# Larger and smaller buffer pools, and a precomputed product spread over more tiles, in a fused attention and two-MLP kernel

## The chip, the cores and the metric

The kernel runs on one core of a Trainium2 chip. Its time is device microseconds, as a median over runs. Everything is one program: an attention step and two MLPs over 4352 tokens, in float32.

## The reference, cut to what matters

```python
# attention: x [8, 8, 512, 64], state [8, 8, 32, 64]
a  = softmax(x @ state^T / 8);      xread = a @ state        # tokens read the state
a2 = softmax(state @ x^T / 8);      sread = a2 @ x           # the state reads the tokens
x  = concatenate([xread, sread], axis=2)                     # -> [4352, 512]
# first MLP, w_in [512, 2048], w_out [2048, 512]
h = x @ w_in
g = where(h >= 1, h, where(h <= -1, 0, (h + 1)**2 / 4))
x = g @ w_out
# second MLP, the same sizes
h = x @ w_in2
g = maximum(h, 0) + alpha * minimum(h, 0)
return g @ w_out2
```

The weights arrive as float64, and the kernel turns their words into float32 itself. Most matrix products are made of three matmuls each: both operands are split into a high part (a cast on ACT) and a low part (a subtraction on DVE), and high x high, high x low and low x high are added up in PSUM.

## The kernel before, in words

**First MLP.** Tokens are worked in nine tiles: tile t below 8 holds the 512 tokens of batch t, tile 8 the 256 rows that the state has read. A tile has 16 steps, one for each 128 columns of the hidden layer; step number i is 16 t + f. In step i the code issues the hidden-layer matmuls of step i + 2 (`h_mm`, L560), the activation on ACT and DVE, and the output matmuls of step i (`out_mm`, L602). All other work hangs on step numbers through `at(i, ...)` (L992): the attention of the next batch, weights and transfers.

For tokens that read the state, the hidden layer is not x @ w_in but attention weights times V, where V = state @ w_in is made ahead: 32 rows for each batch and head. V is made for two groups of batches: batches 1 to 4 during tile 0 (`vg_dir`, L503), and the later batches' V by `vg_plan` (L1043). That plan has 32 products, one for each of 4 column blocks and 8 heads. Product n hangs on step `start + int(n * per)`, with start at step 32, the first step of tile 2: two steps ahead its weights are loaded on POOL's queue into a 2 KB tile (`vg_load`, L493), one step behind it two matmuls go into a PSUM bank (`vg_mm`, L511), ACT copies the bank to SBUF and SP's queue stores it to DRAM (`vg_out`, L498). Batch by batch V comes back from DRAM (`vr_load`, L520), 8 loads a tile, from eight steps into the tile before on.

The raw x of a batch is loaded twice for each half of the heads: as `x1` (L125, four loads of 128 KB) and as `x2` (L134, one of 512 KB). ACT casts x2 to its high part `x2h` (L232, in `s5`).

From step 36 on the weights of the second MLP are prepared too (`w2_plan`, L1084): every 3.4 steps a raw load of 512 KB, decoding, sums of quarters on POOL, high and low parts, and stores to DRAM on SP's queue (`put`, L667).

**Second MLP.** It uses the seven-product scheme for 2 x 2 blocks (Strassen's in Winograd's form) in both layers. The tokens are worked in five super-tiles of two halves of 448 or 416 tokens. For each, the hidden layer comes first (56 units of 6 matmuls: 8 column blocks by 7 products), then the product stage of the output (56 units of 6 matmuls), with a few units of either interleaved at the seams (`second`, L932). The raw input of the next super-tile is loaded in units 4 to 7 of the product stage (`xr_load`, L728; four loads, each of two 128-row slices side by side), combined in place by four subtractions or additions (`x_comb`, L736) and split into high and low parts (`x_split`, L745), from unit 11 on. The seven products of the output need 8 slices each, a high and a low part of 448 columns in one 4 KB tile (`o_split`, L831). The code asks for slice m + 5 in unit m; the first product's 8 slices and 4 of the second's are made during the hidden layer. A slice is free again after its second unit; the first two slices of a product after its third unit.

**Buffers and order.** `U` tiles (128 x 512 words, 2 KB in each partition) come from one pool of 72, `V` tiles (4 KB) from a pool of 14 (L43 and L44). V tiles hold x, x2h and x2l, raw weights, put buffers, the raw input `xr`, slices `gs` and output tiles `ot`. The order on each engine is made when the program is built: of the instructions that are ready the earliest in the code goes first, and a tile is given a buffer when one is free. On the chip every engine and SP's queue work through their list in that order.

Of the kernel before, what the change touches and what calls it, by code (L numbers as in the profile page):

```python
# [14 lines left out]
ALU = mybir.AluOpType  # L15
# [24 lines left out]
@with_exitstack  # L40
def kernel_body(ctx: ExitStack, tc: tile.TileContext, x, state, w1i, w1o, w2i, w2o, alpha, out):
    nc = tc.nc
    up = ctx.enter_context(tc.tile_pool(name="up", bufs=72))  # L43
    vp = ctx.enter_context(tc.tile_pool(name="vp", bufs=14))  # L44
    cp = ctx.enter_context(tc.tile_pool(name="cp", bufs=1))
    sp = ctx.enter_context(tc.tile_pool(name="sp", bufs=4))
    pa = ctx.enter_context(tc.tile_pool(name="pa", bufs=4, space=bass.MemoryType.PSUM))
# [3 lines left out]
    def U(name, dt=F32):  # L51
        return up.tile([128, 512], dt, tag="u", name=name)

    def V(name, dt=F32):
        return vp.tile([128, 1024], dt, tag="v", name=name)
# [7 lines left out]
    act, dve, pool, pe, ld = nc.scalar, nc.vector, nc.gpsimd, nc.tensor, nc.sync  # L63
# [8 lines left out]
    def hi_(h, raw):  # L72
        act.copy(h, raw)  # L73

    def lo_(l, raw, h, eng=None):
        (eng or dve).tensor_tensor(out=l, in0=raw, in1=h.bitcast(F32), op=ALU.subtract)  # L76
# [18 lines left out]
    xd = dp.tile([NO, 128, TOK], F32, name="xd")  # L95
# [456 lines left out]
    def gi(t, f):  # L552
        return t * NF + f
# [166 lines left out]
    WS, XR, XB, HB, GT, GR, GS, OA, OC, OS = {}, {}, {}, {}, {}, {}, {}, {}, {}, []  # L720
# [4 lines left out]
    def wof(s):  # L725
        return HALF[s]

    def xr_load(s, kh, tk):  # L728
        w = wof(s)
        v = V(f"xr{s}{kh}{tk}")[:, :2 * w]  # L730
        c0 = BASE[s] + tk * w
        ld.dma_start(out=v.rearrange("p (k c) -> p k c", k=2),
                     in_=xd[2 * kh:2 * kh + 2, :, c0:c0 + w].rearrange("k p c -> p k c"))
        XR[s, kh, tk] = v

    def x_comb(s, m):  # L736

        b11, b21, b12, b22 = [XR[s, kh, tk] for tk in range(2) for kh in range(2)]
        x, y, op = {3: (b22, b12, ALU.subtract), 2: (b12, b11, ALU.add),
                    4: (b21, b11, ALU.subtract), 1: (b22, b11, ALU.subtract)}[m]  # L740
        dve.tensor_tensor(out={3: b12, 2: b11, 4: b21, 1: b11}[m], in0=x, in1=y, op=op)

    XAT = [11, 13, 18, 20, 22, 33, 35, 37, 42, 44, 46]

    def x_split(s, p):  # L745
        w = wof(s)
        b11, b21, b12, b22 = [XR[s, kh, tk] for tk in range(2) for kh in range(2)]
        src = {0: b11, 1: b21, 2: b22, 3: b21, 4: b11, 5: b11, 6: b12}[p]
        for kk in range(2):
            h, l = U(f"xh{s}{p}{kk}", F32R)[:, :w], U(f"xl{s}{p}{kk}", F32R)[:, :w]  # L750
            r = src[:, kk * w:(kk + 1) * w]
            hi_(h, r)
            lo_(l, r, h)
            XB[s, p, kk] = (h, l)

    XSTEPS = [(x_split, 0), (x_comb, 3), (x_split, 1), (x_comb, 2), (x_split, 5), (x_comb, 4),
              (x_split, 3), (x_comb, 1), (x_split, 4), (x_split, 6), (x_split, 2)]

    def w1_get(s, q, p):
# [172 lines left out]
    def second():  # L932
# [23 lines left out]
        for n, (kind, s, a, b) in enumerate(ev):  # L956
# [6 lines left out]
            if kind == "h":  # L963
                h_item(s, a, b)
                h_after(s, a, b)
                next(late, None)
                if b == 3:
                    o_split(s, 0, a)
                if b == 6 and a in (1, 3, 4, 6):
                    k = (a - 1) // 2 + a // 4  # L970
                    o_split(s, 1, k)
                    g_comb(k, 4)
            else:
                m = 8 * a + b
                if 12 <= m + 5 < 56:
                    o_split(s, *divmod(m + 5, 8))
                if 8 <= m < 12:
                    g_comb(m - 4, 4)
                if 23 <= m < 31:
                    g_comb(m - 23, 1)  # L980
                if s + 1 < NSUP and 4 <= m < 8:
                    xr_load(s + 1, m % 2, m // 6)
                o_item(s, a, b % 4 // 2, [b // 4 * 4 + b % 2 * 2 + k for k in range(2)])
                if s + 1 < NSUP and m in XAT:
                    fn, arg = XSTEPS[XAT.index(m)]
                    fn(s + 1, arg)
# [5 lines left out]
    def at(i, fn, *a):  # L992
        side[i].append((fn, *a))
# [49 lines left out]
    def vg_plan(g, start, per):  # L1043
        n = 0
        for blk in range(4):
            for h in range(NH):
                o = start + int(n * per)
                at(o - 2, vg_load, g, blk, h)
                at(o + 1, vg_mm, g, blk, h)
                n += 1  # L1050
        at(start - 2, ld_stg, g)
        at(start, st_build, g, 0)
        at(start, st_build, g, 1)
# [4 lines left out]
    for blk in range(4):  # L1058
        for c in range(4):
            at(max(1 + c, 4 * blk - 5 + c), vg_dir, blk, c)  # L1060
    vg_plan(1, gi(2, 0), 1.0)

    for blk in (1, 2, 3):
        for c in range(4):
# [37 lines left out]
    for k in range(4):  # L1102
        at(gi(7, 12), xr_load, 0, k % 2, k // 2)
# [88 lines left out]
```

## Time and profile before

| | us |
|---|---|
| three timed runs | 1413.91, 1421.23, 1421.24 |
| their median | 1421.23 |
| the profiled execution's own time | 1414.61 |
| its span in the trace | 1412.8 |
| PE busy in the span | 1374.0 (97%) |
| DVE busy | 1066.7 (75%) |
| ACT busy | 821.3 (58%) |
| POOL busy | 101.9 (7%) |

The span runs from the first to the last instruction of the program in the trace; the 1.8 us between it and the execution's own time lie outside. PE's busy time is the time in which any matmul is in flight, so it tells where PE starves but not whether it works at its best pace. The clock that was granted to PE is told for each stretch as a share of full speed. Busy shares of DVE, ACT and POOL are means over stages with different limits.

### The profile page before, as it was taken

The page shows a single profiled execution, that of the slowest core. Times are in us where ns is not written, and L with a number is a line of the kernel's source. Part 1 is how long each engine was busy: PE and PEld are TensorE (multiplying, and loading weights), DVE is VectorE, ACT ScalarE, POOL GpSimd, SP SyncE. Part 2 cuts the span into 40 slices and gives each one's busy share as a digit, 9 for nine tenths or more (in the row PEclk, how much of TensorE's full clock was granted, in tenths as well). Part 3 has the DMA queues.
Part 4 walks back from the last instruction along what each step waited for, and adds up shares of the span by engine and source line. Part 5 has one row for each costly group of instructions (what it writes and reads, how often), then busy time and mean ns, then how long its engine had stood idle before and what let it go on. Part 6 is the DMA issues. An engine that isn't in the chain of part 4 may idle for free.

```text
span 1412.8 us, 20324 instructions
## 1 busy us (share of the span) xinstructions
PE 1374.0 (97%) x6596; PEld 1192.7 (84%) x6596; DVE 1066.7 (75%) x1896; ACT 821.3 (58%) x1586; POOL 101.9 (7%) x123
## 2 busy tenths in 40 slices
PE   6799999998999999999999999999999999999998
PEld 4466688886788888888898999899999999999997
DVE  6878596776769797976678796779677868786873
ACT  5567676665677776775565454545454545463552
POOL 1000002231222111112111000000000000000000
PEclk9999999999999999999999999999999999999999
DMA  6898446488875656656777786878677777779765
GB/s 200 308 320 272 121 86 146 124 232 239 214 223 160 170 156 191 175 168 197 263 263 259 250 291 192 263 224 279 202 251 255 237 232 255 257 243 308 227 226 159
DMA packets 295962, 312.28 MB, mean 221 GB/s; under 512 B 144048, under 2 KB 179888, under 8 KB 295856
## 3 DMA queue, kind: packets, MB, share of 16 engines
q1 hardware_dynamic: 255504, 293.09, 65.8%
q0 software_dynamic: 33280, 8.51, 3.2%
q10 hardware_dynamic: 7072, 9.37, 1.9%
q8 instruction: 53, 0.87, 0.3%
q14 instruction: 53, 0.43, 0.1%
HBM read 237.90 MB, written 72.35 MB: 220 GB/s over the span
## 4 chain that ended last, share of the span: by engine, by line
PE 83%; issue 5%; DMA 4%; DVE 3%; ACT 2%; POOL 1%; SPq 1%; POOLq 0%; ACTq 0%; DVEq 0%
PE accB L855 23%; PE hB L780 22%; PE accA L620 18%; PE hA L84 11%; PE accA L612 3%; PE vgp L84 1%; DMA vd<-vgo 1%; PE sr L84 1%; PE sc L84 1%; DMA x<-in_x_dram 1%; DMA w2d<-wo 1%; PE vdp L84 1%; DMA wr_wi<-in_moe_w_in_dram 0%; PE vgp L516 0%; PE et L205 0%
## 5 line engine op out<-in xcount | busy, mean ns | idle before, releaser
L855 PE MATMUL accB<-gs,wv 128*128 128x448 f32 (+1 forms) x1680 | 334.8, 359 | 0.5 <-ACT o L873 0.5
L855 PEld LDWEIGHTS accB<-gs,wv 128*128 128x128 f32 x1680 | 315.1, 188 | 16.5 <-ACT o L873 0.8
L780 PE MATMUL hB<-xh,wu 128*128 128x448 f32 (+1 forms) x1120 | 318.4, 361 | 3.0 <-ACT p L806 0.8
L780 PEld LDWEIGHTS hB<-xh,wu 128*128 128x128 f32 x1120 | 210.2, 188 | 18.4 <-ACT p L806 2.3
L780 PE MATMUL hB<-xl,wu 128*128 128x448 f32 (+1 forms) x560 | 201.3, 359 | 0.0
L73 ACT CAST gs<-c 128x448 fp32r<-128x448 f32 (+1 forms) x200 | 109.1, 556 | 79.1 <-PE accB L855 56.1
L787 ACT ACTIVATE m<-c 128x448 f32<-128x448 f32 (+1 forms) x120 | 68.2, 568 | 118.0 <-DVE c L802 115.3
L588 DVE SCALAR_TENSOR_TENSOR g<-y,hA 128x512 f32<-128x512 f32 (+1 forms) x144 | 93.5, 649 | 51.0 <-ACT y L586 49.9
L76 DVE TENSOR_TENSOR gs<-c,gs 128x448 fp32r<-128x448 f32 (+1 forms) x200 | 114.8, 602 | 5.8 <-ACT gs L73 5.0
L76 DVE TENSOR_TENSOR gl<-g,gh 128x512 fp32r<-128x512 f32 (+1 forms) x128 | 88.7, 693 | 36.0 <-ACT gh L73 28.4
L789 DVE SCALAR_TENSOR_TENSOR c<-m,beta_sb,c 128x448 f32<-128x448 f32 (+1 forms) x120 | 80.9, 674 | 44.7 <-ACT m L787 42.3
L585 ACT ACTIVATE y<-hA 128x512 f32<-128x512 f32 (+1 forms) x144 | 82.3, 572 | 52.8 <-PE hA L84 51.2
L780 PEld LDWEIGHTS hB<-xl,wu 128*128 128x128 f32 x560 | 105.2, 188 | 5.1
L73 ACT CAST gh<-g 128x512 fp32r<-128x512 f32 (+1 forms) x128 | 75.7, 592 | 38.4 <-DVE g L588 34.8
L586 ACT ACTIVATE y<-y 128x512 f32<-128x512 f32 (+1 forms) x144 | 87.6, 608 | 3.9
L829 DVE TENSOR_TENSOR c<-c,c 128x448 f32<-128x448 f32 (+1 forms) x120 | 71.9, 612 | 1.9
L802 DVE TENSOR_TENSOR c<-hB,u 128x448 f32<-128x448 f32 (+1 forms) x80 | 48.5, 607 | 25.5 <-PE hB L780 14.6
L500 ACT COPY vgo<-vgp 128x512 f32<-128x512 f32 x64 | 37.2, 586 | 50.4 <-PE vgp L84 23.7
L612 PE MATMUL accA<-g,wf_w1o 128*128 128x512 f32 x128 | 61.0, 607 | 4.6 <-DVE wf_w1o L405 4.6
L76 DVE TENSOR_TENSOR gs<-m,gs 128x448 fp32r<-128x448 f32 (+1 forms) x80 | 47.0, 601 | 16.2 <-ACT gs L73 16.2
L73 ACT CAST gs<-m 128x448 fp32r<-128x448 f32 (+1 forms) x80 | 43.1, 556 | 25.2 <-PE accB L855 20.4
L612 PEld LDWEIGHTS accA<-g,wf_w1o 128*128 128x128 f32 x128 | 24.4, 193 | 26.2 <-issue 18.8
(961 smaller groups left out, 2820.0 us busy)
## 6 DMA issues: line engine op xcount, KB each, us to landing
wu<-w1d SPq DMA_DIRECT2D x280, 256.0 KB
wv<-w2d SPq DMA_DIRECT2D x280, 256.0 KB
vd<-vgo SPq DMA_DIRECT2D x64, 256.0 KB
vr<-vd SPq DMA_DIRECT2D x56, 256.0 KB
w1d<-wu SPq DMA_DIRECT2D x56, 256.0 KB
w2d<-wo SPq DMA_DIRECT2D x40, 256.0 KB
x<-in_x_dram SPq DMA_DIRECT2D x18, 512.0 KB
wr_wi<-in_moe_w_in_dram SPq DMA_DIRECT2D x16, 512.0 KB
```

Source lines behind the costliest of these rows:

```text
L73: act.copy(h, raw)
L76: (eng or dve).tensor_tensor(out=l, in0=raw, in1=h.bitcast(F32), op=ALU.subtract)
L84: pe.matmul(ps, a, b, start=(k == 0), stop=(k == n - 1))
L585: act.activation(out=y[:, :n], in_=ps, func=AF.Relu, bias=0.5, scale=0.5)
L586: act.activation(out=y[:, :n], in_=y[:, :n], func=AF.Square)
L588: dve.scalar_tensor_tensor(out=g[:, :n], in0=y[:, :n], scalar=1.0, in1=ps, op0=ALU.min, op1=ALU.max)
L612: pe.matmul(ACC[k], w[:, k * 128:(k + 1) * 128], g, start=(f == 0), stop=(f == NF - 1))
L620: pe.matmul(ACC[k][:, :n], a, b, start=(f == 0 and j == 0), stop=(f == NF - 1 and j == 2))
L780: pe.matmul(ps, a[:, kk], b, start=(new and m == 0), stop=(m == 5), skip_group_check=True)
L789: dve.scalar_tensor_tensor(out=g, in0=m, scalar=beta_sb[:, f:f + 1], in1=h, op0=ALU.mult, op1=ALU.add)
L829: dve.tensor_tensor(out=o, in0=x, in1=y, op=op)
L855: pe.matmul(ps, a[:, js], b, start=(new and k == 0 and n == 0), stop=(k == 7 and n == 2), skip_group_check=True)
```

## The change

Three edits. The pools become 80 buffers of 2 KB and 10 of 4 KB (the same memory). The raw input of the second MLP goes into 2 KB tiles: 8 loads of one slice each instead of 4 loads of two, combinations in two halves, and splits that read those tiles. And the later batches' V products stand 1.4 steps apart instead of one, so that the last hangs on step 32 + 43 + 1 instead of 32 + 31 + 1.

```diff
-    up = ctx.enter_context(tc.tile_pool(name="up", bufs=72))
-    vp = ctx.enter_context(tc.tile_pool(name="vp", bufs=14))
+    up = ctx.enter_context(tc.tile_pool(name="up", bufs=80))
+    vp = ctx.enter_context(tc.tile_pool(name="vp", bufs=10))
...
     def xr_load(s, kh, tk):
         w = wof(s)
-        v = V(f"xr{s}{kh}{tk}")[:, :2 * w]
         c0 = BASE[s] + tk * w
-        ld.dma_start(out=v.rearrange("p (k c) -> p k c", k=2),
-                     in_=xd[2 * kh:2 * kh + 2, :, c0:c0 + w].rearrange("k p c -> p k c"))
-        XR[s, kh, tk] = v
+        for k in range(2):
+            t = XR[s, kh, tk, k] = U(f"xr{s}{kh}{tk}{k}")[:, :w]
+            ld.dma_start(out=t, in_=xd[2 * kh + k, :, c0:c0 + w])
 
     def x_comb(s, m):
 
-        b11, b21, b12, b22 = [XR[s, kh, tk] for tk in range(2) for kh in range(2)]
-        x, y, op = {3: (b22, b12, ALU.subtract), 2: (b12, b11, ALU.add),
-                    4: (b21, b11, ALU.subtract), 1: (b22, b11, ALU.subtract)}[m]
-        dve.tensor_tensor(out={3: b12, 2: b11, 4: b21, 1: b11}[m], in0=x, in1=y, op=op)
+        for k in range(2):
+            b11, b21, b12, b22 = [XR[s, kh, tk, k] for tk in range(2) for kh in range(2)]
+            x, y, op = {3: (b22, b12, ALU.subtract), 2: (b12, b11, ALU.add),
+                        4: (b21, b11, ALU.subtract), 1: (b22, b11, ALU.subtract)}[m]
+            dve.tensor_tensor(out={3: b12, 2: b11, 4: b21, 1: b11}[m], in0=x, in1=y, op=op)
...
     def x_split(s, p):
         w = wof(s)
-        b11, b21, b12, b22 = [XR[s, kh, tk] for tk in range(2) for kh in range(2)]
-        src = {0: b11, 1: b21, 2: b22, 3: b21, 4: b11, 5: b11, 6: b12}[p]
+        kh, tk = {0: (0, 0), 1: (1, 0), 2: (1, 1), 3: (1, 0), 4: (0, 0), 5: (0, 0), 6: (0, 1)}[p]
         for kk in range(2):
...
-            r = src[:, kk * w:(kk + 1) * w]
+            r = XR[s, kh, tk, kk]
...
-    vg_plan(1, gi(2, 0), 1.0)
+    vg_plan(1, gi(2, 0), 1.4)
```

## Rows read from the trace of the kernel before

**Rows 1.** The page: busy time by engine, and the chain's shares by engine.

```profile
PE 1374.0 (97%) x6596; PEld 1192.7 (84%) x6596; DVE 1066.7 (75%) x1896; ACT 821.3 (58%) x1586; POOL 101.9 (7%) x123
...
PE 83%; issue 5%; DMA 4%; DVE 3%; ACT 2%; POOL 1%; SPq 1%; POOLq 0%; ACTq 0%; DVEq 0%
```

**Rows 2.** Windows, tiles 2 to 5: stretch, length, busy (instructions) by engine, clock, DMA.

```profile
227.40:306.40 79.00, 78.92 (x368) 65.59 (x366) 56.40 (x101) 54.94 (x105) 18.30 (x22) 1.00 0.63 166
306.40:401.70 95.30, 85.55 (x365) 67.82 (x364) 70.07 (x113) 60.46 (x117) 24.72 (x30) 0.95 0.85 222
401.70:475.30 73.60, 73.53 (x340) 61.04 (x339) 62.14 (x111) 53.48 (x102) 10.93 (x10) 1.00 0.59 177
475.30:547.20 71.90, 71.90 (x334) 59.98 (x333) 62.42 (x111) 52.33 (x98) 9.63 (x10) 1.00 0.62 171
```

**Rows 3.** Windows of 20 us around tile 3's first half.

```profile
300.00:320.00 20.00, 20.00 (x90) 16.53 (x89) 15.28 (x20) 12.73 (x23) 8.03 (x9) 1.00 0.85 217
320.00:340.00 20.00, 18.57 (x81) 14.24 (x80) 13.37 (x24) 13.57 (x26) 3.11 (x4) 1.00 0.92 242
340.00:360.00 20.00, 14.46 (x51) 10.35 (x49) 14.70 (x23) 8.55 (x15) 4.75 (x6) 0.83 0.84 206
```

**Rows 4.** Windows, the second MLP from 780 to 1400 us.

```profile
780.00:1400.00 620.00, 618.53 (x3136) 587.12 (x3135) 463.98 (x812) 306.98 (x607) 0.00 (x0) 1.00 0.75 244
```

**Rows 5.** The chain of waits, 335 to 365 us: start, length, what.

```profile
336.46 10.68 DMA x<-in_x_dram
...
348.11 0.59 ACT vgo L500
...
348.75 0.80 PE vgp L516
```

**Rows 6.** Timeline of SP's queue: start, length, line, what it issues.

```profile
337.38 6.45 SPq L501 DMA_DIRECT2D vd<-vgo  x1
...
349.10 0.43 SPq L138 DMA_DIRECT2D x<-in_x_dram  x1
```

**Rows 7.** Timeline of ACT, casts of x2; in brackets idle before, and releaser.

```profile
347.16 1.04 ACT L73 CAST x2h<-x 128x1024 fp32r<-128x1024 f32 x1 [5.33 <-DMA x<-in_x_dram]
...
362.02 1.04 ACT L73 CAST x2h<-x 128x1024 fp32r<-128x1024 f32 x1 [6.73 <-DMA x<-in_x_dram]
...
426.17 1.05 ACT L73 CAST x2h<-x 128x1024 fp32r<-128x1024 f32 x1 [3.94 <-DMA x<-in_x_dram]
```

**Rows 8.** Tiles ws and vgo: issues (ns min/median/max, first and last), landing.

```profile
L495 POOL DMA_DIRECT2D ws<-wd x32: 776/776/968, 229.4 to 395.0; - x32
...
DMA to landing us min/median/max: 8.4/10.6/14.1
...
L501 SPq DMA_DIRECT2D vd<-vgo x32: 314/332/6448, 243.2 to 414.1; - x32
```

**Rows 9.** Windows, tile vgp alone, tiles 2 to 4: PE, PEld, ACT, clock, DMA.

```profile
227.40:306.40 79.00, 8.04 (x26) 4.75 (x26) 7.65 (x13) 1.00 0.63 166
306.40:401.70 95.30, 10.88 (x32) 5.85 (x32) 9.36 (x16) 0.95 0.85 222
401.70:475.30 73.60, 1.85 (x6) 1.13 (x6) 1.76 (x3) 1.00 0.59 177
```

**Rows 10.** The chain of waits at the first product stage's head.

```profile
810.34 2.43 PE accB L855 x12
...
813.98 8.11 PE accB L855 x40
```

**Rows 11.** The page's costliest groups: slices' casts and subtractions (busy, mean ns, idle before).

```profile
L73 ACT CAST gs<-c 128x448 fp32r<-128x448 f32 (+1 forms) x200 | 109.1, 556 | 79.1 <-PE accB L855 56.1
...
L76 DVE TENSOR_TENSOR gs<-c,gs 128x448 fp32r<-128x448 f32 (+1 forms) x200 | 114.8, 602 | 5.8 <-ACT gs L73 5.0
```

**Rows 12.** Tile xr: loads and combinations (ns min/median/max, first and last start).

```profile
L732 SPq DMA_DIRECT2D xr<-xd x20: 360/424/948, 647.1 to 1219.5; - x20
L741 DVE TENSOR_TENSOR xr<-xr,xr x20: 1011/1083/1092, 660.7 to 1251.0; 128x896 f32<-128x896 f32 x12, 128x832 f32<-128x832 f32 x8
```

## The prediction

> **What bounds the kernel now.** I read the totals first: the tensor engine is busy 97% of the span and the chain that ended last is 83% its own work [rows 1]. So time can only be won where PE is idle or slow, and lost where it newly starves. Next I cut the first MLP into its token tiles, each from its first hidden-layer matmul to the next tile's [rows 2]. Tile 5, which has no V products left in it, takes 71.90 us for 334 matmuls, 0.215 us each. Tile 3 has 365 matmuls; at that pace it would take 78.6 us, but it took 95.30: 16.7 us are lost there. By the same pace tile 2 (368 matmuls, 79.2 against 79.00) and tile 4 (340, 73.2 against 73.60) lose nothing. The 20 us windows show where in tile 3: PE full to 320, 1.4 us idle by 340, then 5.5 us idle with a granted clock of 0.83 [rows 3]. In the second MLP from 780 to 1400 us PE idles 1.5 us in 620 [rows 4]: nothing to win there, a lot to lose.
>
> What happens in tile 3 is read from the chain of waits [rows 5]. A batch load of x lands 10.68 us after its issue at 336.46; ACT then makes its cast and, behind it, a copy of a V product out of PSUM (vgo, 348.11); PE's next V product starts only after that copy. On SP's queue [rows 6] the store of the next V product sits from 337.38 for 6.45 us, and the next x load comes only at 349.10, behind another such store. So it is a ring: ACT waits for x, the V products' copies wait on ACT, their stores wait for the copies on SP, and the next x load waits behind the stores. ACT's casts of x waited 5.33 and 6.73 us in tile 3; in tile 4 one waited 3.94 us [rows 7], and PE lost nothing there.
>
> **The products spread out (1.4 steps apart).** Each of the 32 products issues one load on POOL's queue, two matmuls, one ACT copy and one store on SP [rows 8]. The plan starts at step 32; tile boundaries as I cut them lie two steps ahead of a step's number. At one per step the code puts 13, 16 and 3 products in tiles 2, 3 and 4, and the trace's copies count 13, 16 and 3 [rows 9]. With int(1.4 n) they become 10, 11 and 11 (the last at step 76; the first V tile made of the last block is fetched at step 84, so no consumer gets late). PE's work is only moved: 10 matmuls leave tile 3 and 16 enter tile 4.
>
> What it relieves is the transfers. The DMA engines' share times the tile's length is 0.85 x 95.30 = 81.0 us in tile 3 and 0.62 x 71.90 = 44.6 us in tile 5, so a product's load and store cost about (81.0 - 44.6) / 16 = 2.3 us of transfer time. Against the 78.6 us that tile 3 should last, 81.0 is 1.03: more than fits. Afterwards it is 81.0 - 5 x 2.3 = 69.5 over 76.4 us (355 matmuls), a share of 0.91. Tile 4 goes from 0.59 x 73.60 = 43.4 to 43.4 + 8 x 2.3 = 61.8 over 77.0 us, 0.80. What is left of the stall I read from the nearest windows [rows 3]: at 0.85 no idle time, at 0.92 1.4 us in 20. So tile 3 keeps about 76.4 / 20 x 1.3 = 5 us. Tile 4's mean of 0.80 gives none, but x is loaded at a tile's head and ACT's 3.94 us wait there will grow once stores stand on SP again: 1 us. Gain 16.7 - 6 = 10.7, taken as 10. The ends: nothing is gained (the ring only moves to tile 4), or all 16.7. On the queues it is moved past: tile 4's POOL gets 8 more load issues of 0.78 us beside 10.93 busy, and ACT 8 more copies of 0.59 us beside 53.48 busy of 73.60 [rows 2, 5, 8]; both have room.
>
> **80 buffers of 2 KB.** V product weights are fetched as far ahead as free 2 KB buffers allow; with eight more the loads go out earlier. They land after 8.4 to 14.1 us [rows 8], and PE's stall was on a copy, not on a load [rows 5]. I take 0, bounded by 2 us either way (the trace does not show deeper fetching; one landing's spread over three tiles is the nearest row).
>
> **10 buffers of 4 KB, raw input out of them.** In the first MLP the 4 KB tiles alive are x, its two halves, raw weights and put buffers; by the code's order mostly 5 to 9 at once, and up to 11 at one place in tile 2, where loads and casts stand far ahead of their use; in tile 3 the x loads are held by SP's order [rows 6], not by buffers: 0. In the second MLP the raw input takes 4 of the 14 through most of a product stage, so the slices have 10 left then, as they will have after: 0 there. The one place that loses is the head of each product stage. The code prepares 12 slices before it (8 of the first product, 4 of the second); now 10 fit, and the first product's last two must wait for its third unit to free two buffers. That unit starts at 810.34 and, by 12 matmuls in 2.43 us, ends at 811.55; the two slices are read in the sixth unit, at 813.98 + 1.2 = 815.2 [rows 10]. Two slices take two ACT casts and a subtraction on DVE, 2 x 0.56 + 0.60 = 1.7 us [rows 11]. So 1.9 us are left: hidden, thinly. I take 0; if DVE's queue eats the cover it costs up to about 4 us at each of five stages.
>
> **Raw input in 2 KB tiles.** 20 subtractions of 1.083 us become 40 of half the width; the nearest row, a subtraction 448 wide, is 0.602 [rows 11, 12], so +0.12 us x 20 = 2.4 us of DVE, which is busy 464 of 620 us there [rows 4]: 0 on PE, 2.4 us uncovered. 20 loads become 40 of half the bytes: 20 more issues of 0.424 us on SP [rows 12], 8.5 us in all, taken as 0 because the data is first read several units later; 8.5 is the upper end. No row shows a halved load.
>
> The Trainium skill speaks against this split: "DMA: Bandwidth & Descriptors", section "Rules for kernel authors", says to coalesce small transfers into large ones, and its section "Anatomy of one DMA" puts a fixed cost of about 2.0 us on each (given for the POOL path), so the sum by it would be an estimated 20 x 2.0 = 40 us more if nothing hid it. The trace hides such costs elsewhere: the V loads take 8.4 to 14.1 us and no PE wait in the chain ends on one of them. It counts below as the fourth rival.
>
> **Sum.** Profiled execution 1414.61 us, minus 10, is 1404.6. The three timed runs are 1413.91, 1421.23 and 1421.24; their median is 6.6 above the profiled execution. I carry that offset over: 1411.
>
> **Rivals.**
> First, the ring moves: tile 4 has x loads at its head just as tile 3, and 11 products instead of 3. For it: ACT already waits 3.94 us for x there. Against: a share of 0.80. It keeps 10 to 17 us of loss: 1414 to 1421, no change that can be measured; 1419 as its centre.
> Second, slower: the 4 KB pool. If the two late slices take over 1.9 us longer than worked out (DVE is the engine in doubt), PE idles at the head of each product stage; about 3 us idle, and some 1 us more since the clock was granted at 0.83 in the window that held the tile 3 idles [rows 3]. Five stages cost 20, minus the gain of 10: 1431. For it: ACT's casts of slices already wait for the tensor engine to release buffers, 56.1 us in all [rows 11]. Against: PE stays full today while they do.
> Third, everything goes: the ring needs both a late x load and a full SP queue, and the thinner traffic breaks it altogether: 1404 to 1406.
> Fourth, the halved loads hold SP's queue in front of the weights of the product stage: up to 8.5 us, 1420.
>
> **Chances.** Forecast 0.46 (own range 1406 to 1415), everything goes 0.10, the ring moves 0.28, halved loads 0.05, slower 0.11. A difference of 0.5% is about what can be told from no change here, 7.1 us: faster means under 1414.1, slower over 1428.3. The forecast and the third rival fall under it but for a tenth of the forecast's chance or so, which gives 0.53 faster; the ring, the halved loads and that rest give 0.36 the same; slower keeps 0.11. For 8 times in 10 the range goes from 1400 (all of it gone and the eight buffers' 2 us) to 1424.
>
> **What would show it.** Right: tile 3 near 80 us and tile 4 near 78, products 10, 11 and 11, ACT's waits for x under 4 us, a granted clock of 1.00 from 340 to 380, second MLP unchanged to 2 us. Wrong: tile 4 over 82 us with casts of x waiting over 5 us (the ring moved), or PE gaps after the second pair of units of a product stage, behind slice casts (the 4 KB pool).

## The result, and the profile after

The changed kernel takes 1434.55 us (median of 4 runs, 1433.58 to 1437.68) against 1417.57 for the kernel before on the same chip: a ratio of 1.0124, interval 1.0083 to 1.0166. It is slower by 17 us, where 1411 was predicted and 1424 was the upper end of the range. The profiled execution took 1433.8 us, its span is 1432.0, 19.2 more than before.

The page's totals after (busy time by engine, then the chain's shares) answer to [rows 1]:

```profile
PE 1381.6 (96%) x6596; PEld 1194.6 (83%) x6596; DVE 1068.1 (75%) x1916; ACT 822.3 (57%) x1586; POOL 102.4 (7%) x123
...
PE 69%; DMA 13%; DVE 8%; issue 4%; ACT 3%; POOL 1%; SPq 1%; POOLq 0%; ACTq 0%; DVEq 0%
```

The work is the same, but landings of transfers now make up 13% of the chain, where they were 4%. The windows of tiles 2 to 5 after, columns as in [rows 2]:

```profile
226.82:311.10 84.28, 79.31 (x361) 65.55 (x360) 57.76 (x101) 53.23 (x102) 15.69 (x18) 0.98 0.51 140
311.10:402.17 91.07, 81.92 (x356) 65.82 (x354) 67.03 (x113) 58.36 (x112) 20.91 (x25) 0.94 0.81 199
402.17:489.71 87.54, 81.42 (x356) 65.81 (x354) 62.14 (x111) 57.27 (x110) 16.93 (x19) 0.96 0.74 209
489.71:561.60 71.89, 71.89 (x334) 59.97 (x333) 62.48 (x111) 52.01 (x98) 10.47 (x10) 1.00 0.56 162
```

At the pace of tile 5, 0.215 us a matmul, tile 3 should take 76.5 us and tile 4 as much: they lose 14.5 and 11.0 us. Tile 2 (77.6 at that pace) loses 6.7. Before, only tile 3 lost 16.7. So the stall of tile 3 stayed nearly whole, and two new ones stand beside it. Three windows of 20 us from tiles 3 and 4, and the second MLP (as [rows 3, 4]):

```profile
340.00:360.00 20.00, 12.91 (x45) 9.73 (x44) 11.05 (x21) 11.60 (x22) 0.00 (x0) 0.74 0.83 205
400.00:420.00 20.00, 18.69 (x82) 14.90 (x81) 11.56 (x20) 12.11 (x24) 5.19 (x6) 1.00 0.92 255
420.00:440.00 20.00, 15.76 (x68) 12.46 (x67) 11.66 (x22) 12.33 (x24) 3.95 (x5) 0.94 0.77 205
...
780.00:1400.00 620.00, 618.76 (x3116) 582.51 (x3115) 469.25 (x834) 310.73 (x612) 0.00 (x0) 1.00 0.75 249
```

The second MLP is as full as before. In tiles 3 and 4 PE idles (7.1 us from 340 to 360), and where it has idled the granted clock is lower: from 341 to 346 us it is busy for 0.9 us only, and from 346 to 354 the granted clock is 0.50, which is 1.2 GHz; the window's 0.74 is a mean of stretches at 2.4 and at 1.2 GHz. Of the 14.5 us that tile 3 loses PE idles 9.2 (91.07 - 81.92); in the other 5.4 it is busy for longer than its pace asks (81.92 - 76.5).

What ended ACT's idle time is told by its waits, first of tile 3, then of tile 4 (waiter, what it waited for, us in total, times, longest):

```profile
ACT vw321h L73 <- DMA vr<-vd: 9.7, 1, 9.7
...
ACT vw401h L73 <- DMA vr<-vd: 4.1, 1, 4.1
ACT vgo L500 <- DMA xd<-oA: 3.3, 1, 3.3
...
ACT x2h L73 <- DMA x<-in_x_dram: 1.7, 1, 1.7
...
ACT x2h L73 <- DMA x<-in_x_dram: 8.5, 2, 4.9
ACT gh L73 <- DMA x<-in_x_dram: 5.2, 1, 5.2
...
ACT vw420h L73 <- DMA vr<-vd: 2.7, 1, 2.7
```

In tile 3 ACT hardly waits for x any more ([rows 7] had 5.33 and 6.73 us); it waits for a V tile, 9.7 us, and the tile loses nearly as much as before. In tile 4 its casts of x2 wait for x again, 8.5 us. The 5.2 us before the cast of gh come by a detour: ACT's own store of an output tile (L636) went out only when an x load had landed at 417.23, and the cast stood behind that store.

Tile 2 is another matter. Its chain (start, length, what) has the first product's weights landing after 17.49 us, where the slowest landing before took 14.1 [rows 8]:

```profile
228.85 17.49 DMA ws<-wd
...
246.48 0.61 PE vgp L516
```

SP's queue shows what ran beside it. First after, then before: the third raw weight load of the second MLP goes out at 227.79 in place of 214.21. That is 1.06 us ahead of the issue at 228.85 whose weights took 17.49 us, with two V loads between the two.

```profile
216.11 0.37 SPq L138 DMA_DIRECT2D x<-in_x_dram  x1
227.79 0.34 SPq L381 DMA_DIRECT2D wr_w2o<-in_moe_w_out_dram  x1
228.22 1.23 SPq L524 DMA_DIRECT2D vr<-vd  x2
```

```profile
213.73 0.43 SPq L138 DMA_DIRECT2D x<-in_x_dram  x1
214.21 6.17 SPq L381 DMA_DIRECT2D wr_w2o<-in_moe_w_out_dram  x1
```

By the buffers' order that raw load takes over the 4 KB buffer of an x tile whose last reader ends at 227.8. The rest of the 19.2 us: tiles 7 and 8 together 4.5 more, the second MLP from its first output matmul 1.1 more, tile 6 and the start 1.5 less.

### The profile page after: what moved, and what is told of

Its sections match the earlier page's. It is cut to its first block, busy times and chain, and to the rows that moved or that the text cites. A ratio compares the mean times of both kernels' runs of the same rounds, so it can differ in the third digit from the quotient of the medians.

```text
span 1432.0 us, 20497 instructions
## 1 busy us (share of the span) xinstructions
PE 1381.6 (96%) x6596; PEld 1194.6 (83%) x6596; DVE 1068.1 (75%) x1916; ACT 822.3 (57%) x1586; POOL 102.4 (7%) x123
## 4 chain that ended last, share of the span: by engine, by line
PE 69%; DMA 13%; DVE 8%; issue 4%; ACT 3%; POOL 1%; SPq 1%; POOLq 0%; ACTq 0%; DVEq 0%
PE accB L854 23%; PE hB L779 20%; PE accA L620 11%; PE hA L84 7%; DMA vr<-vd 3%; DMA x<-in_x_dram 3%; PE accA L612 3%; DMA wu<-w1d 2%; PE vgp L84 1%; DMA ws<-wd 1%; DMA vd<-vgo 1%; DMA wr_wi<-in_moe_w_in_dram 1%; DVE gl L76 1%; PE sc L84 1%; DVE g L588 1%
## 5 line engine op out<-in xcount | busy, mean ns | idle before, releaser
L73 ACT CAST gs<-c 128x448 fp32r<-128x448 f32 (+1 forms) x200 | 109.5, 556 | 88.8 <-PE accB L854 69.5
L76 DVE TENSOR_TENSOR gl<-g,gh 128x512 fp32r<-128x512 f32 (+1 forms) x128 | 92.0, 719 | 41.0 <-ACT gh L73 35.4
L788 DVE SCALAR_TENSOR_TENSOR c<-m,beta_sb,c 128x448 f32<-128x448 f32 (+1 forms) x120 | 80.8, 673 | 47.1 <-ACT m L786 45.6
L73 ACT CAST gh<-g 128x512 fp32r<-128x512 f32 (+1 forms) x128 | 75.7, 591 | 48.9 <-DVE g L588 39.6
L586 ACT ACTIVATE y<-y 128x512 f32<-128x512 f32 (+1 forms) x144 | 87.5, 608 | 3.9
```

Of the source, the lines that this page charges most:

```text
L586: act.activation(out=y[:, :n], in_=y[:, :n], func=AF.Square)
L788: dve.scalar_tensor_tensor(out=g, in0=m, scalar=beta_sb[:, f:f + 1], in1=h, op0=ALU.mult, op1=ALU.add)
```

## Experiments

All lengths below are of the profiled executions, cut as above, in us; the ratio is that of the timed runs to the kernel before on the same chip, with its interval. "2nd" runs from the second MLP's first output matmul to the end; in kernels that leave that part alone it lies anywhere from 604.6 to 610.3, so smaller differences in it mean nothing. A tile's length is of one execution, and timed runs of one kernel lie up to 14 us apart (before on one chip: 1411.39 to 1425.38; e9's profiled execution, 1404.9, is its fastest, the median 1409.3). So a difference of a few us in one pair of kernels can be chance; where an edit leaves tile 1 alone, it repeats to 0.1 us.

| kernel | t1 | t2 | t3 | t4 | t7+8 | 2nd | ratio |
|---|---|---|---|---|---|---|---|
| before | 73.8 | 79.0 | 95.3 | 73.5 | 111.3 | 606.3 | |
| after | 73.8 | 84.3 | 91.1 | 87.5 | 115.9 | 607.4 | 1.0124 |
| e1 spread alone | 73.8 | 77.5 | 94.3 | 89.0 | 114.5 | 606.9 | 1.0119 [1.0098, 1.0140] |
| e2 after, no spread | 73.8 | 86.1 | 98.6 | 73.5 | 112.0 | 605.4 | 1.0094 [1.0074, 1.0114] |
| e3 after, old pools | 73.8 | 77.7 | 94.5 | 88.9 | 113.8 | 614.7 | 1.0152 [1.0128, 1.0175] |
| e4 raw input alone | 73.8 | 78.9 | 96.0 | 73.5 | 112.0 | 613.6 | 1.0040 [1.0027, 1.0054] |
| e5 stores on ACT | 73.7 | 83.3 | 94.2 | 74.1 | 111.4 | 608.4 | 1.0020 [1.0003, 1.0037] |
| e6 x2 early | 73.8 | 78.9 | 92.6 | 75.7 | 112.0 | 605.4 | 0.9987 [0.9969, 1.0004] |
| e7 spread, x2 early | 73.8 | 77.7 | 91.0 | 84.6 | 111.2 | 607.7 | 1.0035 [1.0012, 1.0059] |
| e8 after, 76 and 12 | 73.8 | 77.4 | 90.6 | 89.1 | 114.7 | 609.0 | 1.0102 [1.0070, 1.0135] |
| e9 products early | 80.8 | 82.8 | 73.4 | 71.9 | 113.8 | 605.4 | 0.9950 [0.9930, 0.9971] |
| e10 spread, puts late | 73.8 | 77.3 | 78.3 | 76.9 | 116.9 | 608.1 | 1.0034 [1.0014, 1.0053] |
| e11 e9, x2 early | 86.1 | 84.2 | 73.2 | 72.5 | 111.4 | 609.9 | 0.9975 [0.9958, 0.9993] |
| e12 e9, puts from t3 | 80.8 | 86.9 | 73.7 | 71.9 | 112.5 | 606.3 | 0.9956 [0.9937, 0.9976] |
| e13 e12, casts late | 80.9 | 86.5 | 73.4 | 71.9 | 111.2 | 608.9 | 0.9940 [0.9920, 0.9960] |
| e14 after, as e12 | 89.0 | 81.4 | 73.8 | 71.9 | 112.1 | 605.8 | 0.9965 [0.9947, 0.9982] |
| e15 spread, 4 loads | 73.8 | 77.4 | 78.0 | 82.1 | 111.6 | 610.3 | 0.9920 [0.9894, 0.9947] |
| e16 before, 4 loads | 73.8 | 79.0 | 82.4 | 74.1 | 111.3 | 608.6 | 0.9901 [0.9867, 0.9935] |
| e17 e9, casts late | 80.9 | 82.6 | 73.8 | 71.9 | 116.3 | 606.3 | 0.9950 [0.9929, 0.9972] |
| e18 loads on SP | 73.8 | 99.6 | 142.1 | 92.4 | 111.4 | 604.6 | 1.0627 [1.0597, 1.0657] |

### Which edit costs: e1, e2, e3, e4

```diff
# e1, on before (e2 is the same edit undone on after)
-    vg_plan(1, gi(2, 0), 1.0)
+    vg_plan(1, gi(2, 0), 1.4)
# e3, on after (e4 undoes the spread besides)
-    up ... bufs=80;  vp ... bufs=10
+    up ... bufs=72;  vp ... bufs=14
```

> The kernel before with one edit: the 32 products 1.4 steps apart; pools of 72 and 14, raw input in 4 KB tiles. Theory A (the spread itself costs: products and their stores in tile 4 make a new ring there, and their weight loads come late): 1428 to 1436 us, tile 4 at 84 to 88 us, tile 3 at about 91. Theory B (the 4 KB pool of 10 costs: a raw weight load that it pushes from 214 to 227.8 us collides with the first product's load): no slower than before, 1408 to 1420, tile 2 at 79 us and tile 4 under 78.

> The changed kernel with the products put back at one step apart: 80 and 10 buffers, raw input in 2 KB tiles. Theory A: as before within 0.4%, 1413 to 1422, tile 2 at 79 us, tile 3 at 95, tile 4 at 73.5, and the few us of tile 8 stay. Theory B: slower than before by 5 us or more, 1423 to 1432, with a first product that waits some 5 us for its weight load in tile 2.

> The changed kernel with the old pools of 72 and 14 buffers; products 1.4 steps apart and raw input in 2 KB tiles stay. Theory A: as the changed kernel, 1428 to 1436, tile 4 at 84 to 88 us. Theory B: 1410 to 1420, tile 2 back at 79 us. If 72 buffers are too few for the raw input in the second MLP, the second MLP grows by some us besides, which only this run and the next would show.

> The kernel before with raw input in 2 KB tiles alone (pools of 72 and 14, products one step apart). Both theories: the first seven tiles as before to 1 us each, time 1414 to 1423. A third theory (C: the 3.5 us more in tile 8 of the changed kernel come from the raw input's 16 loads on the sync queue instead of 4 to 8): tile 8 up to its first second-MLP matmul grows from 45.9 to about 49 us; without it, it stays at 46.

The spread alone brings the whole loss of tile 4 and relieves tile 3 of nothing but its matmuls' time. The windows of e1's tiles 3 and 4:

```profile
305.10:399.41 94.31, 83.59 (x355) 65.83 (x354) 66.98 (x113) 58.57 (x112) 21.74 (x25) 0.96 0.78 191
399.41:488.45 89.04, 80.44 (x356) 64.88 (x354) 63.00 (x112) 56.97 (x109) 17.26 (x19) 0.98 0.74 208
```

The pools cost too, whatever the spread: 7.1 us in tile 2 between e4 and e2, 6.6 between e3 and after. In the second MLP they give about the same back: the raw input in 2 KB tiles needs the eight further buffers, and without them it takes 7 to 8 us more (e3 and e4). The timed runs say the same less sharply: e4, with the raw input alone, is 0.0040 slower than before, that is 5.7 us, interval 3.8 to 7.6. No run has the 80 buffers without the 10; only the two together were told apart from 72 and 14. The costs don't add up: e2's pools cost 2.6 us more in tile 3, after's took 3.4 off it. Both edits bear on transfers of the same stretch, but differences of this size can also be chance. Theories A and B were both half right; C's mark is met in e4 (tile 8 at 49.4 us), but tile 7 is shorter there by nearly as much: the border only shifted, and the two together take 0.7 more.

### Is it a ring, and what is the tenth buffer: e5, e6, e7, e8

```diff
# e5, on before
-        ld.dma_start(out=vd[g][blk][h], in_=o)
+        (act if g else ld).dma_start(out=vd[g][blk][h], in_=o)
# e6, on before; e7, on e1
-            at(o + 3, ld_x2, b, q)
+            at(o - 1, ld_x2, b, q)
# e8, on after
-    up ... bufs=80;  vp ... bufs=10
+    up ... bufs=76;  vp ... bufs=12
```

> The kernel before with one edit: the stores of the later batches' V products are issued from ACT's queue, right behind the copy that they wait for, and no longer from SP's. Theory D (ring through SP's queue: the store holds SP until the copy is made, the next x load stands behind it, and the copy stands behind ACT's cast of x): x loads go out earlier, ACT's waits for x fall from 5.3, 6.7 and 3.9 us to under 2, tile 3 falls from 95.3 to 79 to 83 us, time 1400 to 1406. Theory E (the transfer time of tile 3 is full, or the transfers are limited by how many are in flight): tile 3 stays over 90 us and the time at 1412 to 1420; ACT then itself waits in front of its stores.

> The kernel before with one edit: the second load of each x half (x2) stands four steps earlier in the program, so in SP's queue it is ahead of four products' stores. Theory D: x2 lands before ACT wants it, ACT's waits for x go to under 1 us, tile 3 falls to 79 to 83 us, time 1400 to 1406. Theory E: the same bytes still share the same time, another operand comes late (a product's weights, a V tile or the x1 half), tile 3 stays over 90 us, time 1412 to 1420. A cost of the edit itself: the tiles stay allocated some 20 us longer, and the pool of 14 could hold SP elsewhere.

> The kernel before with two edits: products 1.4 steps apart (as in the run with the spread alone, 1431 us) and x2 loaded four steps earlier. Theory D: both the stall of tile 3 (94.3 us there) and that of tile 4 (89.0) go, to 77 to 81 and 77 to 80 us; time 1400 to 1406, so the spread was harmful only through x arriving late. Theory E: tile 4 stays over 85 us, time 1425 to 1435.

> The changed kernel with 76 and 12 buffers instead of 80 and 10. Theory F (in tile 2 the tenth 4 KB buffer is what lacks: x2 of batch 3 waits for a buffer until 216 us, SP's queue stands still behind it, a raw weight load of 512 KB goes out at 228 instead of 214 us and meets the first product's weight load, which takes 17.5 us): tile 2 back from 84.3 to 77.5 to 78.5 us, tiles 3 and 4 still at 91 to 95 and 87 to 89; time 1428 to 1433, since tile 3 gives back some of it as in the run with the old pools. Against it: tile 2 stays at 84, and the load was late for another reason.

In e6 no cast of x2 waits at all, and tile 3 still takes 92.6 us. ACT's waits in its tile 3:

```profile
ACT vw321h L73 <- DMA w2d<-wo: 7.6, 1, 7.6
ACT vgo L500 <- DMA vd<-vgo: 6.2, 1, 6.2
ACT vw400h L73 <- DMA vr<-vd: 3.5, 1, 3.5
ACT vw401h L73 <- DMA vr<-vd: 3.2, 1, 3.2
```

Other landings ended the wait: that of a put whose 2 KB buffer a V tile takes over, that of a product's store. In e7 it was ACT's own store of an output tile, whose issue stood until a put had landed (the chain, 403 to 416 us); the output tile was ready at 406.6. In the trace the instruction just before that issue waits for the semaphore which the store itself will raise when it is done, and the put raises the same one: the transfers of SP and of ACT share eight such semaphores in turn (POOL's have eight others), and 1185 of SP's 1188 issues in before's trace wait like this. So it is the program as built that holds the issue; that the chip would hold it is not shown. The lines:

```profile
403.42 11.09 DMA w2d<-wo
...
414.59 0.33 ACTq L636
...
415.23 0.63 ACT gh L73
```

e5, which takes the stores out of SP's queue, left tile 3 at 94.2 and put 4.3 us into tile 2. So theory D fell for tile 3, and its rival E, that tile 3 stays over 90 us, held in both (1418.5 and 1412.9 us). e7 missed both theories: 1420.6 us, some 10.7 under e1, about a third of it from each of tile 3, tile 4 and tiles 7 and 8. The ring was one form that the stall took on, not its cause. The chain of before's own tile 3, of which [rows 5] show one link, has other landings in turn on either side of that x load:

```profile
316.66 8.74 DMA w2d<-wo
...
325.46 6.49 DMA vd<-vgo
...
356.03 6.91 DMA vd<-vgo
```

e8 bears out theory F: with two more 4 KB buffers (and four fewer of 2 KB) that raw load goes out at 215.80 (before: 214.21), and tile 2 is back at 77.4 us. SP and PE work through the first MLP in the same order there as in after, so the order is no rival here.

```profile
215.80 3.24 SPq L381 DMA_DIRECT2D wr_w2o<-in_moe_w_out_dram  x1
```

### Thin out the transfers: e9 to e14, e17

```diff
# e9, on before
-    vg_plan(1, gi(2, 0), 1.0)
+    vg_plan(1, gi(1, 0), 1.0)
# e10, on e1 (e12, on e9, and e14, on after with e9's edit: gi(3, 0) + int(3.0 * n))
-        w2_plan(..., gi(2, 4) + int(3.4 * n))
+        w2_plan(..., gi(5, 0) + int(1.8 * n))
# e11, on e9: e6's edit.  e13, on e12, and e17, on e9:
-        at(gi(7, c + 2), xs_hi, c);  at(gi(7, c + 3), xs_lo, c)
+        at(gi(7, c + 5), xs_hi, c);  at(gi(7, c + 6), xs_lo, c)
```

> The kernel before with one edit: the 32 products start at the head of tile 1 instead of tile 2, one per step, so that they lie in tiles 1 and 2 and are over before most of the second MLP's raw loads and puts begin. Theory G (crowd: in tiles that hold products, puts and x loads together a transfer takes 10 us and more, and ACT, in order, waits for landings of many kinds: x, V tiles, its own stores, puts; removing one kind only lets the next end the wait): tile 1 grows by its 16 products' matmuls to about 80.6 us, tile 2 stays at 79, tile 3 falls to 72 to 74, time 1396 to 1402. The rival H (products cost a stall wherever x loads stand beside them): tile 1 or 2 grows by another 8 to 14 us, time 1408 to 1418.

> The run with the spread alone (1431 us) with one more edit: the 26 weight preparations of the second MLP (raw loads, decoding, put stores) start at the head of tile 5 and come 1.8 steps apart, where they started in tile 2, 3.4 apart; so no put lies beside a product. Theory G: tile 3 falls from 94.3 to 76 to 78 us and tile 4 from 89.0 to 76 to 78; tiles 5 to 7 carry nearly twice the puts and may grow by 0 to 10 us; time 1398 to 1412. Rival H: tiles 3 and 4 stay over 85 us each, time 1425 or more.

> The kernel with the products from tile 1 on, and x2 loaded four steps earlier as well. Theory G: no wait for x ends late once products and puts lie apart, so within 3 us of the run without the second edit. If that run kept a stall in tile 1 or 2 that ends on x, this one is faster by its size.

> The kernel with the products in tiles 1 and 2 (1409 us) with one more edit: the second MLP's 26 weight preparations start at the head of tile 3 and come 3.0 steps apart, not in tile 2 and 3.4 apart. Theory G (products beside puts): tile 2 falls from 82.8 to 78.5 to 80 us, tile 3 from 73.4 to 72 to 73, tiles 4 to 7 stay within 2 us; time 1402 to 1407. Rival H (products beside x loads): tile 2 stays at 82 to 83 us, time 1407 to 1411.

> The same kernel with one more edit: the four casts of the last tile's turned x (xsh) and the subtractions behind them stand three steps later in tile 7. If ACT's wait of 5.4 us for the last of the 16 turning transfers is what costs tile 7 some 2.5 us (67.9 in place of 65.4), that goes: 2 to 3 us under the run without it. If not, within 1 us of it.

> The changed kernel (80 and 10 buffers, raw input in 2 KB tiles) with the products one step apart from the head of tile 1 and the 26 preparations 3.0 apart from the head of tile 3. Theory G with F: nothing of the changed pools' 6 to 7 us of tile 2 is left, since no 512 KB raw load waits for a 4 KB buffer at the first product; tiles 1 to 3 as in the same order with the old pools, within 2 us, and the time within 3 us of it (the second MLP was 0.9 us shorter with these pools). If the pool of 10 costs wherever products run, tile 1 or 2 is 5 us or more longer than with the old pools.

> The kernel with the products from the head of tile 1 on (1409 us) and the last tile's four xsh casts three steps later, puts where they were. Tiles 1 to 3 as there (80.8, 82.8, 73.4 us), tile 7 shorter by 2.5 us as in the pair of runs before: 1405 to 1408. If the order of the transfers falls out otherwise, tile 2 may take 3 us more or less.

e10 keeps the spread and takes the puts away from beside it: tile 3 falls from 94.3 to 78.3 us, tile 4 from 89.0 to 76.9, both nearly at pace. The puts, crowded into tiles 5 to 7, make a stall of their own in tile 6: it takes 84.4 us where e1's took 71.9, more than was allowed for, so the time is 1421.3 us where 1398 to 1412 was expected. Windows of e10's tiles 3, 4 and 6:

```profile
305.00:383.28 78.28, 77.46 (x356) 64.03 (x355) 47.83 (x83) 50.09 (x95) 11.39 (x13) 1.00 0.69 176
383.28:460.15 76.87, 76.87 (x356) 64.11 (x354) 45.98 (x81) 49.53 (x95) 9.51 (x12) 1.00 0.41 119
...
534.89:619.33 84.44, 77.35 (x334) 60.61 (x332) 78.75 (x135) 57.86 (x110) 20.14 (x21) 0.96 0.73 220
```

e9 moves the products into tiles 1 and 2 and beats both kernels, 0.9950 (1409.3 us; theory G had 1396 to 1402, and its rival H 1408 to 1418). Its tiles 1 to 3:

```profile
153.84:234.66 80.82, 80.72 (x360) 64.30 (x359) 54.68 (x96) 60.65 (x112) 14.53 (x18) 1.00 0.69 165
234.66:317.48 82.82, 80.16 (x365) 65.73 (x364) 56.07 (x100) 56.16 (x107) 18.17 (x22) 1.00 0.77 196
317.48:390.92 73.44, 73.44 (x339) 61.01 (x338) 63.76 (x112) 54.57 (x104) 15.19 (x15) 1.00 0.71 188
```

Tile 1 took on its products at full pace, tile 3 is free of its stall, tile 2 lost some 4 us, where H had 8 to 14 in one of the two: G had the tiles nearly right and H the time, and neither is whole. Theory G of e12, that these 4 us come from the first puts, was wrong: with the puts gone from tile 2 (e12, e13) it took 86.5 to 86.9 us, over rival H's 82 to 83 too. Loading x2 earlier (e11) put 5 us into tile 1, and the time is 4.1 us over e9's, where within 3 was expected. With the pool of 10 (e14) tile 1 took 89.0, the condition set down for "it costs wherever products run"; but tile 2 was 5.5 us shorter than e12's and the time, 1411.0 against 1409.7, within the 3 us set down for the other theory. So both were met in part, and what the pool costs in this order stays open. The later casts are undecided: 1.3 us less in tiles 7 and 8 from e12 to e13, 2.4 more from e9 to e17. The early orders' ratios, 0.9940 to 0.9975, have intervals that mostly overlap; that they beat before holds for all, which is best does not show.

### Is it the transfers themselves: e15, e16, e18

```diff
# e15, on e1; e16, on before: in vg_load and vg_mm
+        if h:
+            return
...
-        ws = G.pop(("w", g, blk, h))
+        ws = G["w", g, blk, 0]
# e18, on before
-        pool.dma_start(out=t, in_=wd[blk][:, h * D:(h + 1) * D, :])
+        ld.dma_start(out=t.bitcast(F32), in_=wd[blk][:, h * D:(h + 1) * D, :])
```

> The run with the spread alone (1431 us), but only the first product of each block of eight loads its weights, and the other seven use that tile: 4 loads of 256 KB in place of 32, with matmuls, copies, stores and order as they were (the output is left wrong for the later batches). Theory I (the amount of transfer in a tile): the share of the transfers falls from 0.78 to about 0.72 in tile 3 and from 0.74 to about 0.68 in tile 4, tile 3 from 94.3 to 77 to 87 us, tile 4 from 89.0 to 77 to 82; time 1408 to 1420. Theory J (order alone: copies, stores and casts that wait on one another): tile 3 and tile 4 stay within 3 us of 94 and 89, time 1425 to 1432.

> The kernel before with the same edit (4 product loads in place of 32, later batches' output wrong). Theory I: tile 3's share falls from 0.85 to about 0.75 and tile 3 from 95.3 to 79 to 88 us; time 1400 to 1409. Theory J: tile 3 within 3 us of 95, time 1411 to 1418.

> The kernel before with one edit: the weight loads of the later batches' products go out on SP's queue, not on POOL's; bytes, order and everything else stay. In before's tile 3 the 16 loads take 23.8% of 95.3 us, 1.4 us of all transfer engines each, where a store of the same 256 KB on ACT's queue takes 0.74. Theory I (the transfer time that a tile holds): if the load costs 0.74 us on SP's queue, tile 3 holds some 11 us less, and falls from 95.3 to 82 to 90 us; time 1402 to 1410. Rival K (SP's queue in order): a load waits for a free 2 KB buffer and holds the stores and x loads behind it; tile 2 or 3 grows by 5 us or more, time 1418 to 1435.

With 28 of the 32 loads gone and all other work kept, e15's tiles 3 and 4 (first two lines) lose 1.7 and 5.6 us, where e1 lost 18 and 12.5; e16's tile 3 (third line) loses 3.8 in place of 16.7. Theory I holds, J falls, with e15 at 1406.6 us, a little under the 1408 that I had at the least. The order of instructions moved with the edit, at some 26 to 77 places on each engine in e15 but at 3 to 7 in e16, so e16 is the cleaner test. There ACT's waits for x in tile 3 went from the first of the last two lines (before) to the second, though nothing was done to the x loads. One thing is not separated: 28 tiles of 2 KB are free as well. Eight more such buffers, with four fewer of 4 KB, took only 3.4 us off tile 3 (e3 against after).

```profile
305.08:383.08 78.00, 77.31 (x355) 63.90 (x354) 66.09 (x113) 58.31 (x112) 14.76 (x15) 1.00 0.69 192
383.08:465.23 82.15, 77.65 (x356) 63.86 (x355) 62.17 (x111) 56.41 (x109) 10.58 (x11) 1.00 0.63 193
```

```profile
306.58:388.98 82.40, 80.89 (x365) 65.52 (x364) 66.59 (x113) 60.49 (x117) 15.77 (x16) 1.00 0.72 212
```

```profile
ACT x2h L73 <- DMA x<-in_x_dram: 12.1, 2, 6.7
...
ACT x2h L73 <- DMA x<-in_x_dram: 0.7, 1, 0.7
```

The queues of before's tile 3 (kind, packets, MB, share of 16 engines) say what such a load costs. q0 is POOL's, with the 16 loads; q10 is ACT's, with four stores of 256 KB each:

```profile
q1 hardware_dynamic: 18285, 15.84, 57.3%
q0 software_dynamic: 16550, 4.22, 23.8%
q10 hardware_dynamic: 576, 1.05, 3.1%
```

Of 95.3 us that is 1.42 us of all engines for a load and 0.74 for a store of the same size. In the trace such a load has 128 packets of 2 KB, 117 ns each, and some 910 packets of 4 bytes, which make up a third of its price; a store has 128 packets of 2 KB, 92 ns each, and 16 of 4 bytes. e18 sends the loads through SP's queue, where 2 KB packets took 88 ns and the many small ones are absent. (Its loads also write their tile as float32, where POOL's write float32r; which of the two makes the difference is not separated.) The transfers got much cheaper and the kernel 6% slower; its tiles 2 and 3:

```profile
227.32:326.91 99.59, 86.26 (x367) 69.18 (x366) 58.21 (x103) 55.41 (x105) 5.22 (x6) 0.93 0.34 120
326.91:469.06 142.15, 95.39 (x354) 73.46 (x352) 61.93 (x109) 57.64 (x110) 12.82 (x14) 0.82 0.44 140
```

Tile 3 holds 0.44 x 142.15 = 62.5 us of transfers, 18.5 less than before, and loses 66 us. Rival K, slower through SP's list worked in order, has the direction, at three times its size, but not for the reason set down: the loads themselves stood for 3.5 us in all, and the product stores (L501) for some 24, half of it for ACT's copies of products. What SP and PE waited for in tile 3, the longest waits:

```profile
SPq L501 <- ACT vgo L500: 11.9, 5, 4.8
SPq L524 <- PE accA L620: 7.8, 1, 7.8
```

```profile
PE vgp L516 <- DMA ws<-wd: 18.7, 6, 7.8
```

So a weight load now stands behind stores and V loads that wait, and PE waits for product weights, 18.7 us, of which before's tiles 2 and 3 show nothing. The order on the engines changed in dozens of places too, so this reading is an argument, not a test. What it does show is that a low share guards against nothing: a landing that comes after the instruction that needs it costs time, and here a held queue made it late where elsewhere a crowd did.

The Trainium skill, "DMA: Bandwidth & Descriptors", section "Issuing engine by pattern", gives simple loads to the sync queue. e18 did so: each transfer got cheaper, but the kernel got slower, and here the measurement decides against it.

## Why the prediction was wrong

**The arithmetic of the transfers held, the step from them to the stall failed.** It put 69.5 us of transfers into tile 3 and 61.8 into tile 4; the shares after make 0.81 x 91.07 = 73.8 and 0.74 x 87.54 = 64.8. From this it read "5 us" of loss for tile 3 and "1 us" for tile 4, off two 20 us windows with shares of 0.85 and 0.92. Measured: 14.5 and 11.0. It left out the third window of the same [rows 3], where at a share of 0.84 PE idled 5.5 us, and it counted idle time alone, not the matmuls that take longer at the lower clock. Tiles 3 and 4 make some 19 of the 29 us between the 1404.6 forecast for the profiled execution and the 1433.8 measured: a gain of 10.7, taken as 10, was forecast, and they lost 8.8 more than before. A tile's mean share has no point below which nothing is lost: e1's tile 4 lost 12.5 us at 0.74, e9's tile 3 only 0.4 at 0.71, e18's tile 2 over 20 at 0.34. A stall also lengthens the tile and so lowers its own mean share. Set against the length at pace, as the prediction did, the transfers of after's tiles 3 and 4 come to 0.96 and 0.85, e16's tile 3 to 0.75 (3.8 us lost), e9's to 0.71 (0.4 lost): in these rows more means more lost. But after's tile 2, at 0.55 with its late raw load, and e18's at 0.43 break the row, so it is a pattern and not a rule. Two windows inside one stall could not give that scale. This step is where the sign went wrong: of the loss of 16.7 us in one tile 14.5 stayed, and 11.0 came up in the next. The number of products in each tile came out as forecast (10, 11, 11), and so did their cost: 1.42 + 0.74 = 2.16 us for a load and a store priced as ACT's are, where the prediction had 2.3.

**The ring was a form, not the cause.** "ACT waits for x, the copies wait on ACT" was true of before's tile 3, but with x2 there in time (e6) the stall shrank by 2.8 us and with the stores elsewhere (e5) by 1.1. ACT has several kinds of instruction that wait for landings, and when transfers are late the next one ends the wait. The first rival (the ring moves to tile 4) saw the place: tile 4 over 82 us, casts of x waiting 4.94 us. The wait is just under the 5 us that the prediction had set as its mark. It priced it as a move; it was a second copy, and tile 3 kept its own.

**10 buffers of 4 KB.** "Up to 11 at one place in tile 2" was counted and then taken as 0. That place cost 6.6 to 7.1 us (e3 against after, e4 against e2; e8 undoes it). The second rival, slower at 1431, came near the time by luck, on another road: the heads of the product stages where it put its loss run as before.

**80 buffers and the raw input.** Each taken as 0; together they are, within what can be told in the second MLP. Apart they are not: the halved raw input costs 7 to 8 us with 72 buffers in the profiled executions, near the 8.5 named as its upper end, and the larger pool pays for that. The Trainium skill, "DMA: Bandwidth & Descriptors", section "Anatomy of one DMA", has a fixed cost of about 2.0 us for each transfer, from which the prediction worked out an estimated 40 us. No run shows it adding up; the largest growth that the split makes is those 8 us. (What the prediction calls V loads of 8.4 to 14.1 us are the products' weight loads of [rows 8].)

**Tiles 7 and 8.** Nothing was forecast, 4.5 us were lost. e1 has 3.2 of them, e4 0.7. ACT's cast of the last tile's turned x waits 5.6 us there for its transfers, but moving it settled nothing. With x2 loaded early the two tiles take 111.2 and 111.4 us (e7, e11) where the same kernels without that edit take 114.5 and 113.8 (e1, e9); why is not shown, and the cause stays open.

## What to carry to other kernels

When an in-order engine has several kinds of instruction that wait for transfers, the wait seen in the trace is only the one that came last: before building on it, ask which landing would end it next. Spreading work that brings transfers over more of a kernel need not thin a stall if the stretch it goes to already carries others; move it to where transfers are few (tile 1, share 0.45), as the products early did. And a pool's peak counts even where it lasts a moment: here a load that went out 13.6 us later for want of a buffer ran beside one that a matmul needed, and that one took 17.5 us.

## What was not expected of the hardware

The same 256 KB cost the transfer engines 1.42 us as a load on POOL's queue and 0.74 as a store on ACT's. The load's 2 KB packets took longer, 117 ns against 92, and some 910 packets of 4 bytes came with each load. In e18's tile 2, on SP's queue, the 2 KB packets of the same loads took 88 ns and had no such company.

A transfer's issue can also stand until another transfer has landed that it has nothing to do with: in e7 a store on ACT's queue went out 8 us after its data was ready, and the casts behind it on ACT waited with it. As said there, the traces show this as the work of shared semaphores in the program as built. It is one more form of the wait, and nothing here shows it of the chip itself.
